# A gated linear recurrence with a squared-ReLU layer on one core: K and Q laid out in runs for the last four units, K~ and v gathered in 16-row pieces, and the chain's steps ranked first

## The chip, the core and the metric

The kernel runs on one NeuronCore of a Trainium2 chip. TensorE (PE) multiplies matrices into PSUM; VectorE (DVE) and ScalarE (ACT) work on SBUF and PSUM; GpSimd (POOL) makes masks and issues DMAs from its queue; SyncE (SP) issues DMAs. Time is what the device needs for one execution, in microseconds, as the median of several runs. The three runs of the kernel before took 705.7, 706.53 and 707.09 us; the median is 706.53.

## The reference

```python
# 4 batches, 8 heads, 768 steps, 48 columns a head
scale = np.minimum(mag, 0.999) / (mag + 1e-06)       # mag = |a_re + i a_im|
for t in range(S):
    new_re = ar * S_re - ai * S_im                    # a complex decay for each row of the state
    new_im = ar * S_im + ai * S_re
    kv = np.einsum('bhd,bhe->bhde', k[:, :, t], v[:, :, t])
    S_re, S_im = (new_re + kv, new_im)
    y[:, :, t] = np.einsum('bhd,bhde->bhe', q[:, :, t], S_re)
# the heads of a step stand side by side: x has 3072 tokens of 384
h = x @ w_in                                          # 384 x 2048
r = np.maximum(h, 0.0)
g = r * r
out = g @ w_out                                       # 2048 x 384
```

All of it is float32 to the caller; the kernel gets the two weight matrices as 64-bit words and turns them into float32 itself.

## The kernel before, in words

The 3072 steps are six units of 512 (n = 0 to 5), so a unit may begin a batch (n = 0, 3), end one (n = 2, 5), or cross from one to the next (n = 1, 4). A unit has three parts.

*The chain.* `chain(n)` turns the recurrence into attention: it scales a, multiplies it up over all steps (`inner`, `totals`, `scan`, `back`; PE turns the data with `turned`, ACT copies it out of PSUM), and `apply` makes from the running products P the rows Q~ = q P and K~ = k / P, real and imaginary part side by side, 96 numbers a head. A partition then holds four neighbouring steps (step mod 4 is c), heads and columns beside them. DVE does most of it. `gather` copies K~ by DMA from this layout into `KC`, one step a partition, four blocks of 128 steps; `load` brings v in the same way into `vv`. `places(i)` says at which partitions a block's steps stand: blocks with odd i have their two halves of 64 exchanged. From n = 2 (`EARLY`) on, all these DMAs are issued by POOL, one or two a block.

*The pairs.* `pairs(n)` takes two heads at a time, four pairs a unit. From n = 2 on, `turn` transposes Q~ and K~ on DVE (two `transpose` calls of 768 columns, in 32 x 32 blocks, written so that the 128 steps of a block stand in order of time, that is, c innermost), and twelve DMAs move the pieces into `QT`, 96 rows of columns. For n = 0 and 1, `turn_pe` does this on PE. `score` multiplies K by Q on PE for each head, block by block and in halves of 64 K steps, and DVE multiplies the result by the causal mask (`mask4`) into `As`. `keep` multiplies K~ with v (PE) and adds up the states at the block ends (ACT and DVE). `mix` adds masked scores times v and states times Q in PSUM (`ypair`); ACT copies it to `yts`, and SP's DMAs put it into `xT`, tokens in columns.

*The dense layer.* `dense(n, grp)` takes 256 tokens: PE multiplies by w_in (line L1400, `part_of`), ACT takes ReLU and square (L1431, L1432), PE multiplies by w_out (L1446 for n = 0, L1497 after it; from n = 1 on with fewer products and sums on DVE, L1512 and L1521), POOL stores the rows. In unit 0 the weights are still coming: `fetch` loads a piece (POOL's queue, L795), `convert` makes float32 of it (ACT L809 and L813, DVE L815, L819, L822).

The order of everything is planned when the program is built. `Plan.add` takes a step with its engine, an assumed duration, what it reads and writes, and a rank (smaller goes first); `Plan.order` plays this through with one free time per engine, an issue time and a latency per DMA, and emits the steps in the order that comes out. On the chip each engine runs its own list strictly in that order. Ranks: the pairs of unit n (1, n), the chain (2, n), dense work and stores (3, n), v (3, 6 + n); what empties a PSUM bank of the dense layer has (0, n). So dense work of unit n - 1 fills PE while the chain of unit n runs on DVE.

Lines that matter: L1262 the transposes, L1267 their DMAs, L1226 the gathers of K~, L892 the loads of v, L1305 the scores, L1308 the masking, L1334 and L1348 the states, L1359 and L1363 the mix, L993 the chain's turns, L1151 to L1189 `apply`.

Of the kernel before, what the change touches and what calls it, by code (L numbers as in the profile page):

```python
# [598 lines left out]
def fast_path(ctx, tc, q, k, v, a_re, a_im, moe_w_in, moe_w_out, out, flag):  # L599
# [73 lines left out]
    mask = sb("mask", 2 * C)  # L673
# [29 lines left out]
    mask4 = mask.rearrange("p (o t) -> p o t", o=2).unsqueeze(1).to_broadcast([C, W // 2, 2, C])  # L703
# [26 lines left out]
    SCORE = 0.7  # L730
    checked = []

    def step(*args, **kw):
        return plan.add(*args, **kw)
# [63 lines left out]
    def convert(i):  # L798
# [12 lines left out]
        if mixed:  # L811

            step("ACT", 1.92, keys + [("lo", i)], [("lo", i, 1)], lambda: act.activation(  # L813
                out=part(F16, 1), in_=part(I16, 3), func=AF.Copy, scale=2.0 ** -60), rank)
# [44 lines left out]
    def places(i):  # L859
        return [(CH, 0, CH), (0, CH, CH)] if i % 2 else [(0, 0, C)]  # L860

    def load(n):
# [23 lines left out]
        for i in range(W):  # L886
            b, s = divmod(n * L + i * C, S)
            src = v[b, :, s:s + C, :].rearrange("h t d -> t h d")
            for p0, t0, m in places(i):
                vrank = (CHAIN, 1) if n == 1 else (DENSE, 6 + n)  # L890
                dma(pool, [("xT", (n - (vs(n) == vs(n - 1))) % 2, NM - 1)] if n else [("gate",)], [("v", vs(n))],
                    lambda i=i, p0=p0, t0=t0, m=m, src=src: pool.dma_start(  # L892
                        out=t[p0:p0 + m, i], in_=src[t0:t0 + m]), vrank, m * 1536, 4.0,
                    group=n)

    def chain(n):
# [90 lines left out]
        def turned(src, put, by, keys, rk):  # L987
# [6 lines left out]
            step("PE", 0.12 * NM, keys, [(b,)], go, rk)  # L994
# [125 lines left out]
        check("DVE", 0.16, [("tot",)], [("lv", n)], level, ahead)  # L1120
# [93 lines left out]
    def gather(n, z, p, np):  # L1214
# [5 lines left out]
        for i in needs(n):  # L1220
            for p0, t0, m in places(i):
                queue = sp if n < EARLY and i % 2 else pool
                t0, m4 = 32 * i + t0 // W, m // W
                dma(queue, keys, [(k_, z, q_) for q_ in range(p, p + np)
                                  for k_ in ("KC", "KC%d" % (i == 3))],
                    lambda i=i, p0=p0, t0=t0, m=m, m4=m4, queue=queue: queue.dma_start(  # L1226
                        out=kc[p0:p0 + m, i], in_=nat[t0:t0 + m4]),
                    rank, m * w * 4, group=(n, p))

# [10 lines left out]
    def pairs(n, which):  # L1240
# [9 lines left out]
        def turn(i):  # L1250
# [5 lines left out]
            for j in range(2):  # L1256
                nat = ff[z][:, j * Z:(j + 1) * Z].rearrange(
                    "p (c h j r) -> p c h j r", c=W, h=HH, j=NJ)[:, :, ts(i % 2, 2)]
                dst = T6[:, i % 2].rearrange("p j (k h t c) -> p k c h j t", k=2, h=2, c=W)
                step("DVE", tt(768), [("f", z, 2 * j), ("f", z, 2 * j + 1)],  # L1260
                     [("a", z) if i % 2 == 0 else ("qk", z)],
                     lambda nat=nat, dst=dst, j=j: dve.transpose(out=dst[:, j], in_=nat), rank)  # L1262
# [28 lines left out]

        def score(i, h):
            s = got["T", i]
            T = QT[s].rearrange("p (i k h t) -> p i k h t", i=W, k=2, h=2)[0:R]
            b = "sc%d" % take("sc", 2)
            sa = bank[b].rearrange("p (j t) -> p j t", j=W)
# [3 lines left out]
            def go():  # L1300
                for j0 in range(0, W, 2):
                    for half in range(2):
                        for j in (j0, j0 + 1):
                            p0, t0 = CH * (half ^ (j % 2)), CH * half
                            pe.matmul(sa[p0:p0 + CH, j, t0:C], lhsT=T[:, j, 1, h, t0:t0 + CH],  # L1305
                                      rhs=T[:, j, 0, h, t0:C], start=True, stop=True)
            step("PE", SCORE, [("QT", s, h)], [(b,)], go, rank, slack=True)
            step("DVE", tt(L) + 0.05, [(b,)], [("A", a)], lambda: dve.tensor_tensor(  # L1308
                out=As[a].rearrange("p (j o t) -> p j o t", o=2, t=C),
                in0=bank[b].rearrange("p (j o t) -> p j o t", o=2, t=C), in1=mask4,  # L1310
                op=ALU.mult), rank)

        def keep(i):
# [10 lines left out]
            for js in ([j for j in need if j < 3], [j for j in need if j == 3]):  # L1324
# [14 lines left out]
                for j in js:  # L1339
# [6 lines left out]
                    else:  # L1346
                        step("DVE", tt(2 * D) + 0.04, reads, writes,
# [3 lines left out]
        def mix(i):  # L1351
            T = QT[got["T", i]].rearrange("p (i k h t) -> p i k h t", i=W, k=2, h=2)[0:R]
# [3 lines left out]
            def go():  # L1356
                for j in range(W):
# [331 lines left out]
```

## Time and profile before

| | |
|---|---|
| median of three runs | 706.53 us |
| profiled execution, its own time | 706.77 us |
| its span | 705.0 us |
| mean granted clock of TensorE | 0.991 |
| PE, DVE, ACT, POOL busy | 630.2, 557.3, 339.5, 96.3 us |
| DMAs that POOL issues for K~ (L1226) and v (L892, both forms) | 52 and 36 |
| mean DMA traffic | 113 GB/s |

The profile is of one execution. A group of instructions is shown by line, engine, operation and shape, with its busy time, the mean duration of one in nanoseconds, and the idle time of its engine just before it with what ended it. PE's matmuls overlap, so their single durations are longer than their distance; a float32 matmul stands in the profile as two passes, so that one `matmul` call of the code counts as two instructions. The chain that ended last gives starts, lengths and lines in order of time. Waits are listed as who waited for whom, the microseconds in total, how often, and the longest.

### The profile page before, as it was taken

The numbers are of one execution on the slowest core, as the hardware profiler recorded it, in microseconds if no ns is written. First come the engines' busy times: TensorE is split into PE (matmuls) and PEld (weight loads), VectorE is DVE, ScalarE is ACT, GpSimd is POOL, SyncE is SP. The second block draws the span as 40 slices with busy tenths as digits, with TensorE's granted clock in tenths as the row PEclk, the third lists the DMA queues.
The fourth block names the chain that finished last, engine by engine and source line by source line (L and its number), as shares of the span: only waits on it lengthen the run. The fifth ranks groups of instructions, "written<-read, shape, count | busy, mean of one in ns | idle before, by whom it ended". The sixth has DMA issues, their size and how long they took to land.

```text
span 705.0 us, 11855 instructions
## 1 busy us (share of the span) xinstructions
PE 630.2 (89%) x4442; PEld 559.2 (79%) x4442; DVE 557.3 (79%) x1125; ACT 339.5 (48%) x586; POOL 96.3 (14%) x166
## 2 busy tenths in 40 slices
PE   0108898999999999989999999999999999999996
PEld 0007775686778999978998898988899988999996
DVE  7999992989787897885999698988887998336721
ACT  6678736865675153336453438435247352032230
POOL 6301140201100010120021030011030011032200
PEclk9999999999999999999999999999999999999999
DMA  9924386111630006562027580045561035287600
GB/s 285 332 99 101 68 224 191 24 45 45 169 98 5 12 16 156 145 168 68 13 66 185 138 178 8 1 101 146 135 164 18 23 92 141 51 279 253 240 3 27
DMA packets 52068, 79.53 MB, mean 113 GB/s; under 512 B 7745, under 2 KB 35073, under 8 KB 52001
## 3 DMA queue, kind: packets, MB, share of 16 engines
q0 software_dynamic: 11712, 40.90, 19.2%
q1 hardware_dynamic: 36160, 32.79, 18.8%
q10 hardware_dynamic: 4128, 4.98, 2.8%
q8 instruction: 37, 0.61, 0.4%
q14 instruction: 31, 0.25, 0.1%
HBM read 48.76 MB, written 4.72 MB: 76 GB/s over the span
## 4 chain that ended last, share of the span: by engine, by line
PE 61%; DVE 26%; DMA 6%; ACT 3%; issue 2%; SPq 1%; ACTq 0%; DVEq 0%
PE d L1400 21%; PE d L1497 20%; PE d L1446 5%; DVE aq L1262 4%; PE sc L1305 4%; DVE f L1189 3%; DMA aq<-in_q_dram 3%; DVE f L1151 3%; PE yp L1359 3%; PE tr L1334 2%; PE yp L1363 2%; DVE g L1512 2%; DVE aq L1155 2%; DVE KC L1038 1%; DMA QT<-aq 1%
## 5 line engine op out<-in xcount | busy, mean ns | idle before, releaser
L1400 PE MATMUL d<-xT,w 128*128 128x256 f32 x1056 | 237.7, 382 | 2.9 <-DMA xT<-yt 2.9
L1400 PEld LDWEIGHTS d<-xT,w 128*128 128x128 f32 x1056 | 199.6, 191 | 30.6 <-DMA xT<-yt 3.3
L1497 PE MATMUL d<-w,g 128*128 128x192 f32 x832 | 144.2, 329 | 0.0
L1497 PEld LDWEIGHTS d<-w,g 128*128 128x128 f32 x832 | 136.0, 191 | 2.1 <-issue 1.3
L1431 ACT ACTIVATE g<-d 128x512 f32<-128x512 f32 x88 | 52.4, 596 | 129.0 <-PE d L1400 111.2
L1432 ACT ACTIVATE g<-g 128x512 f32<-128x512 f32 x96 | 60.6, 631 | 3.0
L1512 DVE TENSOR_TENSOR g<-g 128x512 f32<-128x512 f32 x56 | 37.7, 687 | 30.6 <-ACT g L1432 18.6
L1497 PE MATMUL d<-T,g 128*128 128x192 f32 x336 | 59.6, 330 | 0.0
L1497 PEld LDWEIGHTS d<-T,g 128*128 128x128 f32 x336 | 56.0, 193 | 0.3
L1226 POOL DMA_DIRECT2D KC<-f x52 | 27.6, 545 | 174.9 <-DVE f L1189 125.3
L1458 POOL DMA_DIRECT2D out_dram<-ot x22 | 12.3, 559 | 278.1 <-DVE ot L1521 247.4
L1446 PE MATMUL d<-w,g 128*128 128x384 f32 x128 | 45.5, 505 | 3.1 <-DVE w L822 3.1
L1262 DVE STREAM_TRANSPOSE aq<-f 128x768 f32<-128x768 f32 x32 | 47.5, 1573 | 0.3
L1151 DVE TENSOR_TENSOR f<-aq,xn 128x384 f32<-128x384 f32 (+1 forms) x64 | 45.5, 749 | 1.4 <-ACT xn L1102 1.4
L1371 ACT COPY yt<-yp 112x512 f32<-112x512 f32 x24 | 13.9, 581 | 63.1 <-PE yp L1363 55.7
L1308 DVE TENSOR_TENSOR A<-sc,mask 128x512 f32<-128x512 f32 x45 | 29.8, 685 | 12.5 <-PE sc L1305 12.2
L1446 PEld LDWEIGHTS d<-w,g 128*128 128x128 f32 x128 | 24.4, 197 | 18.7 <-DVE w L822 3.7
L1305 PEld LDWEIGHTS sc<-QT 96*64 96x64 f32 x736 | 34.1, 137 | 5.6 <-issue 3.3
L1305 PE MATMUL sc<-QT 96*64 96x128 f32 (+1 forms) x736 | 37.4, 250 | 0.6 <-DMA QT<-aq 0.3
L964 DVE TENSOR_TENSOR f<-aq 128x384 f32<-128x384 f32 x72 | 36.9, 552 | 0.8
L1521 DVE TENSOR_TENSOR ot<-ot,d 128x192 f32<-128x192 f32 x61 | 20.7, 348 | 20.0 <-PE d L1497 19.7
L1359 PE MATMUL yp<-A,v 128*48 128x128 f32 x320 | 32.4, 277 | 3.5 <-DVE A L1308 3.3
(179 smaller groups left out, 919.5 us busy)
## 6 DMA issues: line engine op xcount, KB each, us to landing
QT<-aq SPq DMA_DIRECT2D x128, 64.0 KB, 2.0
f<-in_moe_w_in_dram POOLq DMA_DIRECT2D x8, 768.0 KB, 6.8
f<-in_moe_w_out_dram POOLq DMA_DIRECT2D x8, 768.0 KB, 6.8
out_dram<-ot POOLq DMA_DIRECT2D x22, 192.0 KB, 2.4
QT<-aq ACTq DMA_DIRECT2D x64, 64.0 KB, 2.1
KC<-f POOLq DMA_DIRECT2D x36, 96.0 KB, 3.4
xT<-yt SPq DMA_DIRECT2D x36, 96.0 KB, 2.6
aq<-in_a_re_dram SPq DMA_DIRECT2D x8, 384.0 KB, 4.1
```

The costliest lines, as they stand in the source:

```text
L964: lambda c=c, j=j: dve.tensor_tensor(out=f[j], in0=a[:, :, :, c - 1], in1=a[:, j, :, c].unsqueeze(1).to_broadcast([C, 2, HH, D]), op=ALU.m ...
L1151: lambda j=j, r=r: dve.tensor_tensor(out=f4[:, j, r], in0=a[:, r], in1=over(j), op=ALU.mult), late[z])
L1262: lambda nat=nat, dst=dst, j=j: dve.transpose(out=dst[:, j], in_=nat), rank)
L1305: pe.matmul(sa[p0:p0 + CH, j, t0:C], lhsT=T[:, j, 1, h, t0:t0 + CH], rhs=T[:, j, 0, h, t0:C], start=True, stop=True)
L1308: step("DVE", tt(L) + 0.05, [(b,)], [("A", a)], lambda: dve.tensor_tensor(out=As[a].rearrange("p (j o t) -> p j o t", o=2, t=C), in0=bank[ ...
L1359: pe.matmul(ypair[64 * h:64 * h + D, ts(j, C)], lhsT=v5[:, j, 2 * i + h], rhs=aa[h][:, j], start=True, stop=at[j] is None)
L1400: pe.matmul(ps, lhsT=w1[:, f // FP, m, ts(f % FP, C)], rhs=xT[:, n % 2, m, ts(grp, G)], start=(m == 0), stop=(m == NM - 1))
L1431: act.activation(out=o, in_=ps, func=AF.Relu)
L1432: act.activation(out=o, in_=o, func=AF.Square)
L1446: pe.matmul(ps, lhsT=gt[:, f % 2, ts(i, C)], rhs=w2[:, f], start=(f == 0), stop=(f == NF - 1))
L1497: pe.matmul(bank[b][:, 0:DH], lhsT=g4[:, r, j], rhs=w(j), start=first and j == 0, stop=last and j == NT - 1)
L1512: step("DVE", tt(4 * C), gk(x0, h) + gk(x1, h), gk(o, h), lambda: dve.tensor_tensor(out=g4[:, o, sl], in0=g4[:, x0, sl], in1=g4[:, x1, sl] ...
```

## The change

For n = 2 to 5, `turn` writes Q of a head as (c, t), where t is step div 4 and c is step mod 4, 32 neighbouring numbers at a time, and K as (half, c, 16 steps), 16 neighbouring numbers at a time, with K first and one `transpose` for each of its two heads. PE reads K as it stands, so the rows of a score block are in K's new order, and reads Q with a step of 32 columns, so that the columns of scores and outputs stay in order of time (`columns`). v and the gathered K~ must stand in K's order too: `places` now gives eight pieces of 16 rows a block, each a DMA of its own. A second mask in that order is made once, by four matmuls of the first mask with a permutation (`swap`, `causal`) and a copy on ACT; for n = 2 to 5 the masking uses it. Steps of `apply`, `totals`, `back`, `turned` and `keep` that are not DVE's get rank (-1, n), ahead of all else, except the pairs of n = 0. Nine planned durations change (masking, conversion on ACT, the chain's turns, `level`, `mix`, scores, the states' sums, ReLU and square, w_out's products); they alter the order alone.

```diff
@@ -670,7 +670,8 @@
...
     perm = sb("perm", C)
-    mask = sb("mask", 2 * C)
+    masks = sb("mask", 4 * C)
+    mask = masks[:, 0:2 * C]
     NS = 14
...
@@ -700,7 +701,12 @@
...
                                fill=0.0, base=-(p0 ^ (CH * o)), channel_multiplier=-1)
-    mask4 = mask.rearrange("p (o t) -> p o t", o=2).unsqueeze(1).to_broadcast([C, W // 2, 2, C])
+    TQ = CH // W
+    swap = As[0][:, C:2 * C]
+    pool.tensor_copy(out=swap.rearrange("p (o c t) -> p o t c", o=2, c=W),
+                     in_=ident.rearrange("p (o t c) -> p o t c", o=2, c=W))
+    mask4 = [m.rearrange("p (o t) -> p o t", o=2).unsqueeze(1).to_broadcast([C, W // 2, 2, C])
+             for m in (mask, masks[:, 2 * C:4 * C])]
     dve.memset(ypair, 0.0)
...
@@ -727,11 +733,15 @@
...
     SUM = 0.22
-    SCORE = 0.7
+    SCORE = 0.72
     checked = []
 
-    def step(*args, **kw):
-        return plan.add(*args, **kw)
+    FIRST = ("apply", "totals", "back", "turned", "keep")
+
+    def step(eng, dur, reads, writes, fn, rank, *args, **kw):
+        if eng != "DVE" and any(x in fn.__qualname__ for x in FIRST) and rank >= (PAIR, 1):
+            rank = (-1, rank[1])
+        return plan.add(eng, dur, reads, writes, fn, rank, *args, **kw)
 
...
@@ -856,8 +866,10 @@
...
 
-    def places(i):
-        return [(CH, 0, CH), (0, CH, CH)] if i % 2 else [(0, 0, C)]
+    def places(i, n):
+        if n >= EARLY:
+            return [(CH * (o ^ (i % 2)) + TQ * c, c, TQ * o, TQ) for o in range(2) for c in range(W)]
+        return [(CH, 0, 0, CH), (0, 0, CH, CH)] if i % 2 else [(0, 0, 0, C)]
 
...
@@ -885,12 +897,14 @@
...
             b, s = divmod(n * L + i * C, S)
-            src = v[b, :, s:s + C, :].rearrange("h t d -> t h d")
-            for p0, t0, m in places(i):
-                vrank = (CHAIN, 1) if n == 1 else (DENSE, 6 + n)
-                dma(pool, [("xT", (n - (vs(n) == vs(n - 1))) % 2, NM - 1)] if n else [("gate",)], [("v", vs(n))],
-                    lambda i=i, p0=p0, t0=t0, m=m, src=src: pool.dma_start(
-                        out=t[p0:p0 + m, i], in_=src[t0:t0 + m]), vrank, m * 1536, 4.0,
+            src = v[b, :, s:s + C, :]
+            vrank = (CHAIN, 1) if n == 1 else (DENSE, 6 + n)
+            src = (src.rearrange("h (c t) d -> c t h d", c=1) if n < EARLY else
+                   src.rearrange("h (t c) d -> c t h d", c=W))
+            for p0, c, t0, m in places(i, n):
+                dma(pool, [("xT", (n - (vs(n) == vs(n - 1))) % 2, NM - 1)] if n else [("gate",)],
+                    [("v", vs(n))], lambda i=i, p0=p0, t0=t0, m=m, c=c, src=src: pool.dma_start(
+                        out=t[p0:p0 + m, i], in_=src[c, t0:t0 + m]), vrank, m * 1536, 4.0,
                     group=n)
...
@@ -1218,16 +1232,30 @@
...
         for i in needs(n):
-            for p0, t0, m in places(i):
+            for p0, c, t0, m in places(i, n):
                 queue = sp if n < EARLY and i % 2 else pool
-                t0, m4 = 32 * i + t0 // W, m // W
+                if n >= EARLY:
+                    src = nat[32 * i + t0:32 * i + t0 + m, c]
+                else:
+                    src = nat[32 * i + t0 // W:32 * i + (t0 + m) // W]
                 dma(queue, keys, [(k_, z, q_) for q_ in range(p, p + np)
                                   for k_ in ("KC", "KC%d" % (i == 3))],
-                    lambda i=i, p0=p0, t0=t0, m=m, m4=m4, queue=queue: queue.dma_start(
-                        out=kc[p0:p0 + m, i], in_=nat[t0:t0 + m4]),
+                    lambda i=i, p0=p0, m=m, src=src, queue=queue: queue.dma_start(
+                        out=kc[p0:p0 + m, i], in_=src),
                     rank, m * w * 4, group=(n, p))
...
 
+
+    def causal():
+        for o in range(2):
+            for p0 in (0, CH):
+                pe.matmul(bank["tr0"][p0:p0 + CH, ts(o, C)],
+                          lhsT=swap[:, p0 ^ (CH * o):(p0 ^ (CH * o)) + CH], rhs=mask[:, 0:C],
+                          start=True, stop=True)
+
+    step("PE", 0.6, [("A", 0)], [("tr0",)], causal, (CHAIN, -1))
+    step("ACT", ac(2 * C), [("tr0",)], [("mask",)], lambda: act.copy(
+        out=masks[:, 2 * C:4 * C], in_=bank["tr0"][:, 0:2 * C]), (CHAIN, 0.2))
 
...
@@ -1253,13 +1281,18 @@
...
             T6 = aq[z].rearrange("p (y j x) -> p y j x", y=2, j=NJ)
-            for j in range(2):
+            for j in (1, 0):
                 nat = ff[z][:, j * Z:(j + 1) * Z].rearrange(
-                    "p (c h j r) -> p c h j r", c=W, h=HH, j=NJ)[:, :, ts(i % 2, 2)]
-                dst = T6[:, i % 2].rearrange("p j (k h t c) -> p k c h j t", k=2, h=2, c=W)
-                step("DVE", tt(768), [("f", z, 2 * j), ("f", z, 2 * j + 1)],
-                     [("a", z) if i % 2 == 0 else ("qk", z)],
-                     lambda nat=nat, dst=dst, j=j: dve.transpose(out=dst[:, j], in_=nat), rank)
+                    "p (c h j r) -> p c h j r", c=W, h=HH, j=NJ)
+                parts_ = [(nat[:, :, ts(i % 2, 2)], T6[:, i % 2].rearrange(
+                    "p j (k h c t) -> p k c h j t", k=2, h=2, c=W)[:, 0])] if not j else [
+                    (nat[:, :, 2 * (i % 2) + h], T6[:, i % 2].rearrange(
+                        "p j (k h o c t) -> p k h c j o t", k=2, h=2, o=2, c=W)[:, 1, h])
+                    for h in range(2)]
+                for src, dst in parts_:
+                    step("DVE", tt(384 if j else 768), [("f", z, 2 * j), ("f", z, 2 * j + 1)],
+                         [("a", z) if i % 2 == 0 else ("qk", z)],
+                         lambda src=src, dst=dst: dve.transpose(out=dst, in_=src), rank)
             for b in range(W):
...
@@ -1289,11 +1322,16 @@
...
 
+        def columns(s):
+            t6 = QT[s].rearrange("p (i k h %s) -> p i k h t c" % ("t c" if n < EARLY else "c t"),
+                                 i=W, k=2, h=2, c=W)[0:R]
+            return t6[:, :, 0], QT[s].rearrange("p (i k h t) -> p i k h t", i=W, k=2, h=2)[0:R, :, 1]
+
         def score(i, h):
             s = got["T", i]
-            T = QT[s].rearrange("p (i k h t) -> p i k h t", i=W, k=2, h=2)[0:R]
+            qt, kt = columns(s)
             b = "sc%d" % take("sc", 2)
-            sa = bank[b].rearrange("p (j t) -> p j t", j=W)
+            sa = bank[b].rearrange("p (j t c) -> p j t c", j=W, c=W)
             a = take("A", 3 if 0 < n < ROOM else 2)
...
@@ -1301,13 +1339,13 @@
...
                         for j in (j0, j0 + 1):
-                            p0, t0 = CH * (half ^ (j % 2)), CH * half
-                            pe.matmul(sa[p0:p0 + CH, j, t0:C], lhsT=T[:, j, 1, h, t0:t0 + CH],
-                                      rhs=T[:, j, 0, h, t0:C], start=True, stop=True)
+                            p0, t0 = CH * (half ^ (j % 2)), CH // W * half
+                            pe.matmul(sa[p0:p0 + CH, j, t0:], lhsT=kt[:, j, h, ts(half, CH)],
+                                      rhs=qt[:, j, h, t0:], start=True, stop=True)
             step("PE", SCORE, [("QT", s, h)], [(b,)], go, rank, slack=True)
-            step("DVE", tt(L) + 0.05, [(b,)], [("A", a)], lambda: dve.tensor_tensor(
+            step("DVE", tt(L), [(b,), ("mask",)], [("A", a)], lambda: dve.tensor_tensor(
                 out=As[a].rearrange("p (j o t) -> p j o t", o=2, t=C),
-                in0=bank[b].rearrange("p (j o t) -> p j o t", o=2, t=C), in1=mask4,
+                in0=bank[b].rearrange("p (j o t) -> p j o t", o=2, t=C), in1=mask4[n >= EARLY],
                 op=ALU.mult), rank)
...
@@ -1344,12 +1382,13 @@
...
                     else:
-                        step("DVE", tt(2 * D) + 0.04, reads, writes,
+                        step("DVE", tt(2 * D), reads, writes,
                              lambda o=o, j=j, ps=ps: dve.tensor_tensor(
...
         def mix(i):
-            T = QT[got["T", i]].rearrange("p (i k h t) -> p i k h t", i=W, k=2, h=2)[0:R]
+            qt, _ = columns(got["T", i])
+            y4 = ypair.rearrange("p (j t c) -> p j t c", j=W, c=W)
             at, s = got["S", i]
...
@@ -1360,9 +1399,9 @@
...
                         if at[j] is not None:
-                            pe.matmul(ypair[64 * h:64 * h + D, ts(j, C)], lhsT=at[j][:, h],
-                                      rhs=T[:, j, 0, h], start=False, stop=True)
-            step("PE", 2.0, [("A", got["A", i, h]) for h in range(2)]
+                            pe.matmul(y4[64 * h:64 * h + D, j], lhsT=at[j][:, h],
+                                      rhs=qt[:, j, h], start=False, stop=True)
+            step("PE", 1.68, [("A", got["A", i, h]) for h in range(2)]
                  + [("v", vs(n)), ("QT", got["T", i], 0), ("QT", got["T", i], 1),
```

More of the change, by code (lines that the diff above doesn't have):

```diff
@@ L811, in convert @@
         if mixed:
[L813 removed]
+            step("ACT", 1.65, keys + [("lo", i)], [("lo", i, 1)], lambda: act.activation(
                 out=part(F16, 1), in_=part(I16, 3), func=AF.Copy, scale=2.0 ** -60), rank)
@@ L1119, in level @@
                               scalar2=None, op0=ALU.mult)
-        check("DVE", 0.16, [("tot",)], [("lv", n)], level, ahead)
+        check("DVE", 0.26, [("tot",)], [("lv", n)], level, ahead)
         def squares(j):
@@ L1432, in relu @@
                 act.activation(out=o, in_=o, func=AF.Square)
-            step("ACT", 2 * ac(2 * G), [(b, "x"), (b,), (b, "y")],
+            step("ACT", 2 * ac(2 * G) + 0.1, [(b, "x"), (b,), (b, "y")],
                  [(b,)] + [("g", s, r) for r in range(4)], relu, (0, n))
```

4 lines of the change are left out of this document (2 added, 2 removed).

## The prediction

> **What bounds the kernel now.** I read the page first: span, busy shares, and the 40 slices.
>
> ```profile
> span 705.0 us, 11855 instructions
> PE 630.2 (89%) x4442; PEld 559.2 (79%) x4442; DVE 557.3 (79%) x1125; ACT 339.5 (48%) x586; POOL 96.3 (14%) x166
> PE   0108898999999999989999999999999999999996
> ```
>
> TensorE (PE) hardly works in the first three slices (the first chain runs on VectorE), and is nearly full from there to the end. So after about 58 us only three things can move the end: PE's amount of work, PE's idle time, and its clock. The table by stages says how much idle time there is (second pair of numbers: PE busy; the column PEclk: granted clock).
>
> ```profile
> 58.00:140.00 82.00, 75.61 (x535) 58.41 (x534) 66.83 (x118) 54.80 (x89) 14.54 (x21) 0.98 0.51 129
> 140.00:300.00 160.00, 159.18 (x1144) 137.69 (x1144) 134.03 (x290) 82.70 (x153) 13.85 (x26) 1.00 0.29 77
> 300.00:320.00 20.00, 17.11 (x163) 14.96 (x160) 16.46 (x29) 7.74 (x12) 5.08 (x7) 0.93 0.72 175
> 380.00:400.00 20.00, 17.96 (x196) 15.96 (x195) 13.56 (x25) 9.03 (x16) 0.00 (x0) 1.00 0.63 156
> 460.00:500.00 40.00, 37.35 (x293) 33.17 (x292) 32.70 (x42) 17.95 (x31) 4.77 (x9) 0.98 0.52 131
> 500.00:580.00 80.00, 80.00 (x525) 74.34 (x525) 72.89 (x146) 39.94 (x70) 8.90 (x14) 0.99 0.31 80
> 580.00:600.00 20.00, 18.42 (x200) 16.51 (x199) 16.95 (x28) 3.95 (x7) 2.12 (x4) 1.00 0.56 137
> ```
>
> In the units that the change touches (n = 2 to 5, from about 260 us on) PE is idle for 2.89 + 2.04 + 2.65 + 1.58 = 9.2 us; the clock below 1 costs another 0.07 x 20 + 0.02 x 40 + 0.01 x 80 = 3.0 us. Between 58 and 140 us it is 6.4 idle and 1.6 of clock. That is all that a faster VectorE (DVE) can give back: about 12 us. Who ends these waits is in the list of waits and in PE's timeline:
>
> ```profile
> PE yp L1359 <- DVE A L1308: 3.3, 5, 1.6
> PE d L1446 <- DVE w L822: 3.1, 1, 3.1
> PE d L1400 <- DMA xT<-yt: 2.9, 1, 2.9
> PE tr L1334 <- ACT St L1344: 2.6, 2, 1.7
> ```
>
> **The transposes.** Groups of instructions by shape; behind the first bar stand their busy us and the mean ns of one:
>
> ```profile
> L1262 DVE STREAM_TRANSPOSE aq<-f 128x768 f32<-128x768 f32 x32 | 47.5, 1573 | 0.3
> L1189 DVE TENSOR_TENSOR f<-f,aq 128x768 f32<-128x768 f32 x16 | 14.6, 951 | 0.1
> L1082 DVE TENSOR_TENSOR KC<-e,yt 128x384 f32<-128x384 f32 x24 | 12.3, 551 | 0.2
> L1087 DVE TENSOR_TENSOR xn<-KC 128x384 f32<-128x384 f32 x12 | 9.7, 810 | 0.4
> L1226 POOL DMA_DIRECT2D KC<-f x52 | 27.6, 545 | 174.9 <-DVE f L1189 125.3 <-issue 21.5 <-PE sc L1305 18.3
> L892 POOL DMA_DIRECT2D v<-in_v_dram x30 | 22.8, 767 | 38.9 <-issue 35.3 <-DMA g<-in_moe_w_in_dram 2.3 <-DMA w<-in_moe_w_in_dram 1.3
> L813 ACT ACTIVATE w<-w 128x768 f16<-128x768 int16 x5 | 9.4, 1926 | 0.0
> L822 DVE CUSTOM_DVE_ANT_0 w<-T,w 128x1536 uint16<-128x1536 uint16 x5 | 4.8, 959 | 0.3
> ```
>
> A transpose of 768 columns (L1262) takes 1573 ns where other DVE work of that size takes 951; its destination has the mod-4 step innermost, so consecutive elements land four floats apart. L1087 shows the same thing without a transpose: 384 elements written 16 floats apart take 810, against 551 (L1082) written in a row. So a far-stepped write costs (1573 - 951)/768 = 0.81 or (810 - 551)/384 = 0.67 ns an element. After the change Q is written in runs of 32 and K in runs of 16: I take 0.95 us for Q and two of 0.55 for K (one instruction more per pair), 2.05 instead of 3.15 us a pair: 1.1 us less, 4.4 a unit, 17.6 over 16 pairs. Bounds: no gain, if transposing itself is the 1573, and 17.6. They are on DVE's path to scores and sums, so each unit's pairs can end some 4 us sooner. The DMAs into QT (12 of 64 KB a pair, on SP and ACT) are as many as before, and wait for all three transposes.
> The Trainium skill ("SBUF — State Buffer", section "Door 1: The DMA port swizzle") says that SBUF has 16-byte lines, and that an access that goes to a new line pays. The two strided rows agree for DVE's writes.
>
> **Reading Q by PE.** Scores and state products now read Q 32 floats apart inside each four; PSUM is written in natural order. No row shows PE reading far-stepped data. Bounds: nothing, or DVE's surcharge. PE's strided side that is in the trace, L1285, writes PSUM four floats apart:
>
> ```profile
> 169.65 0.87 PE tr L1285 x8
> 402.43 1.34 PE sc L1305 x32
> ```
>
> Eight passes of 128 columns in 0.87 us are 0.85 ns a column, no more than the 0.84 of the contiguous products below. I take nothing, as it is the same engine; the other end is priced with the rivals. The page's rule names no engine, and speaks for that other end.
>
> **POOL's queue.** A gather of K~ was 1 or 2 DMAs a block, now 8: 4, 6, 4, 4 issues per half of the heads become 24, 32, 24, 24, so 36 become 208; v goes from 24 to 128. At 545 and 767 ns that is 172 x 0.545 + 104 x 0.767 = 174 us more on an engine busy for 96. The bytes stay. What waits behind them:
>
> ```profile
> 262.99 2.23 POOL L1226 DMA_DIRECT2D KC<-f  x4 [11.07 <-issue]
> 283.48 2.18 POOL L1226 DMA_DIRECT2D KC<-f  x4 [18.26 <-PE sc L1305]
> 363.51 3.13 POOL L1226 DMA_DIRECT2D KC<-f  x6 [3.97 <-DVE f L1189]
> KC<-f POOLq DMA_DIRECT2D x36, 96.0 KB, 3.4
> KC<-f POOLq DMA_DIRECT2D x16, 192.0 KB, 3.3
> 310.07 2.86 PE L1400 MATMUL d<-xT,w 128*128 128x256 f32 x12
> 408.24 10.60 PE d L1497 x64
> ```
>
> The work behind the last K~ is sums and the last mix; I give it the 5.8 us that now lie between the last score (402.43, above) and the end of the last mix (408.2, where w_out's products go on). n = 3 is the tightest: 363.5 + 32 x 0.545 = 381 for the first half of the heads, 398.4 for the second, landed by 401.8, last mix over at 407.6: just within what it is now. For n = 2 the second half lands at 283.5 + 24 x 0.545 + 3.4 = 300, its last mix is over at 306, now at 310.1; n = 4 and 5 have as many issues as n = 2. So nothing is lost against now, and only part of DVE's 4 us can be cashed in n = 3. The cover is DVE's own work on the second half and PE's dense products; without it the 13 to 17 us of a half would stand on the path. v is issued one unit ahead, 24.5 us in which POOL has little else (one store of a row block may wait behind it): covered, with one exception.
>
> **The exception: v of n = 2.** In the built order its 32 issues stand ahead of the last five fetches of w_out (QT, QT, w, T, T), which wait behind them.
>
> ```profile
> 89.31 4.65 POOL L892 DMA_DIRECT2D v<-in_v_dram  x6 [6.00 <-issue]
> 93.95 1.44 POOL L795 DMA_DIRECT2D QT<-in_moe_w_out_dram  x2
> QT<-in_moe_w_out_dram POOLq DMA_DIRECT2D x2, 768.0 KB, 10.3
> 111.40 7.90 PE L1446 MATMUL d<-w,g 128*128 128x384 f32 x24
> 122.43 4.54 PE L1446 MATMUL d<-w,g 128*128 128x384 f32 x8 [3.13 <-DVE w L822]
> 250.25 19.43 PE d L1400 x90
> ```
>
> The first fetch slips from 93.95 to 89.3 + 24.5 = 113.8, lands by about 124, and is converted by two steps on ACT and two on DVE (L813 1.93, L822 0.96, and two shorter ones): some 4 us, 128. PE needed that piece at 119.3 and got it at 122.4. The built order now gives PE 24 passes of L1400 ahead of it (19.43/90 each: 5.2 us, to 124.5), where 12 stood behind it before. Before, 119.3 to 129.4 held 20 passes worth 5.2 us, 5 us lost; after, a wait of 2 to 4 us and some clock. I take 0, bounds -2 to +4.
>
> **The ranks and the rest.** The chain's PE and ACT steps go ahead of others; the built order shows it in unit 0, where the second half's L1172 to L1189 move ahead of two conversion steps. PE waits 1.14 us there:
>
> ```profile
> 81.99 2.14 PE L1285 MATMUL d<-ident,f 128*96 128x128 f32 x16 [1.14 <-DVE f L1189]
> 315.82 4.62 PE L1400 MATMUL d<-xT,w 128*128 128x256 f32 x13 [2.89 <-DMA xT<-yt]
> 5.21 0.84 ACT L914 ACTIVATE f<-aq 128x768 f32<-128x768 f32 x1 [3.12 <-DMA aq<-in_a_re_dram]
> ```
>
> I take -1 (bounds 0 and -1.5). The second mask adds a copy on POOL, four matmuls on an idle PE, and an ACT copy at the head of ACT's queue, where everything of ACT waits behind it; ACT waits for a_re until 5.21 anyway: 0, at worst +0.7. Every score's masking now also waits for that copy, done 250 us earlier. The changed planned times add no instruction; they only order.
> Units 2 to 5: the stalls inside the pairs (2.04 + 2.65 + 1.58 and the clock's 1.6 beside them, 7.9) are waits for masking, sums and QT, which DVE now delivers some 4 us sooner in each unit; I let them go but for a rest of 1, and the late one is then K~ on POOL. The 2.89 at 315.8 is the way from the last mix through yt to xT; the built order still leaves PE no w_out product behind the last mix of n = 2, and now none in n = 5 either (16 matmuls before): one such wait stays, one of 2.9 comes. Net -7.9 + 1 + 2.9 = -4. Bounds: -12.2 (all goes) and +5.8 (nothing goes, two such waits come).
>
> **Sum.** 705.0 + 0 - 1 - 4 = 700 us of span. The profiled execution was 706.77, 1.8 over its span, and 0.2 over the median 706.53: 701.5 us.
>
> **The rivals.**
> (1) PE reads Q slowly. Columns of n = 2 to 5: 32 scores of 16 passes, 1536 columns, and 112 state products of two passes of 128: 77,800. Two stand side by side (the row of 1.34 us has 32 passes of 96 columns on average, 0.44 ns each), so half of it counts: 38,900 x 0.67 to 0.81 = 26 to 32 us, all on a full PE: 728 to 734. For it: two strided DVE rows. Against: PE's own strided row is free. By the page's line rule the same columns pay, and the time is this rival's. 0.2.
> (2) POOL becomes the bound, the other way round. If 16-row gathers cost v's 767 instead of 545 ns, n = 3's last K~ lands at 363.5 + 64 x 0.767 + 3.4 = 416, its last mix ends at 422 instead of 408, 13 us later, with only 24 passes of L1497 left over in the built order (10.60/64 each: 4 us); the other units lose their gain: 705 - 1 + 9 + 1.8 = 715. It decides from 0.56 us an issue on (408.2 - 5.8 - 3.4 - 363.5 = 35.5 over 64). For it: v's DMAs, in small pieces, do take 767. Against: 545 holds for 96 as for 192 KB, and K~'s rows stay in one piece each. 0.14.
> (3) The transposes do not get faster, or the fixed order keeps PE's stalls where they are: 705 to 708. 0.12.
> The forecast: 0.54.
>
> **The numbers.** Own range of the likeliest: 705 + 1.5 - 12.2 - 1.5 - 2 = 691 at best; its unfavourable bounds lead into (3). The range 692 to 716 takes in (3) and (2), and leaves out (1) and the extremes. Within 0.2% (1.4 us) is what this kernel's measurement can hardly tell from no change. Faster: 0.54 and a third of (3), 0.58; same 0.09; slower: (1), (2) and a part of (3), 0.33.
>
> **What would show it.** Transposes at 0.95 and 0.55 us (if not: the step on DVE is wrong). L1305's and L1363's successors at 1.34 us per 32 passes as before (if above 2: rival 1). POOL near 270 us busy, gathers at 545 ns, v at 767, K~ of n = 3 landed some 38 us after its first issue. PE's idle time from 300 to 600 near 5 instead of 9.2 us, with waits left for xT and KC. From 110 to 140 us PE loses as much as now. Wrong would be any price on PE's reads, and any wait that a slow POOL makes at the sums.

## The result

The changed kernel takes 731.28 us (median of four runs, 729.03 to 734.33), against 706.79 us for the kernel before beside it: the ratio is 1.035, with a 95% interval of 1.0318 to 1.0382. It is slower by 3.5%, where 701.5 us was predicted. The profiled execution took 730.35 us, with a span of 728.6.

The page of the changed kernel, its busy shares and PE's 40 slices:

```profile
span 728.6 us, 12280 instructions
PE 660.5 (91%) x4450; PEld 575.3 (79%) x4450; DVE 544.5 (75%) x1141; ACT 339.8 (47%) x587; POOL 227.0 (31%) x443
PE   0008899999999999989999999999999999999996
```

DVE has 12.8 us less to do and POOL 130.7 us more, but neither is what grew with the span: PE is busy for 30.3 us more with eight instructions more (the second mask), and the span is 23.6 longer. The table by stages (length, then busy us of PE, its weight loads, DVE, ACT and POOL; granted clock, DMA share, GB/s) shows that PE has hardly any idle time left where it had most:

```profile
58.00:140.00 82.00, 77.59 (x554) 60.77 (x553) 71.48 (x136) 57.66 (x97) 27.18 (x48) 1.00 0.53 128
140.00:300.00 160.00, 159.51 (x1102) 136.42 (x1101) 123.63 (x272) 80.36 (x146) 33.45 (x67) 1.00 0.28 78
300.00:320.00 20.00, 19.40 (x171) 16.08 (x171) 13.68 (x25) 4.37 (x7) 5.10 (x10) 1.00 0.35 89
320.00:340.00 20.00, 18.52 (x90) 16.03 (x89) 16.42 (x54) 14.66 (x30) 12.20 (x24) 1.00 0.51 116
340.00:500.00 160.00, 160.00 (x1065) 144.04 (x1064) 131.24 (x257) 72.41 (x129) 69.26 (x141) 1.00 0.37 89
500.00:620.00 120.00, 120.00 (x832) 107.03 (x833) 91.34 (x186) 46.26 (x82) 46.15 (x93) 1.00 0.33 84
```

From 300 to 620 us PE is idle for 0.6 + 1.5 = 2.1 us, and its clock is 1.00 throughout. The stalls went as hoped, and more so. What takes longer is PE's own work, and the groups by shape say which. First the kernel before, then the changed kernel:

```profile
L1305 PE MATMUL sc<-QT 96*64 96x128 f32 x368 | 34.2, 279 | 0.6 <-DMA QT<-aq 0.3 <-ACT QT L1288 0.2
L1305 PE MATMUL sc<-QT 96*64 96x64 f32 x368 | 27.2, 221 | 0.0
L1363 PE MATMUL yp<-QT,St 96*48 96x128 f32 x248 | 25.7, 272 | 0.0
L1359 PE MATMUL yp<-A,v 128*48 128x128 f32 x320 | 32.4, 277 | 3.5 <-DVE A L1308 3.3
...
L1343 PE MATMUL sc<-QT 96*64 96x128 f32 x368 | 52.5, 371 | 0.0
L1343 PE MATMUL sc<-QT 96*64 96x64 f32 x368 | 35.9, 272 | 0.0
L1402 PE MATMUL yp<-QT,St 96*48 96x128 f32 x248 | 36.2, 359 | 0.0
L1398 PE MATMUL yp<-A,v 128*48 128x128 f32 x320 | 34.4, 280 | 2.0 <-DVE A L1346 2.0
L1295 DVE STREAM_TRANSPOSE aq<-f 128x384 f32<-128x384 f32 x32 | 16.9, 554 | 0.2
L1295 DVE STREAM_TRANSPOSE aq<-f 128x768 f32<-128x768 f32 x16 | 15.1, 942 | 0.0
```

The two groups that read Q as moving data (scores L1343, state products L1402) have longer passes; the masked scores times v (L1398), which stand between the state products and read contiguously, hardly change (280 ns against 277). The chain that ended last (start, length, work) shows it beside a place where Q is still read contiguously:

```profile
414.46 0.57 PE yp L1398 x8
415.04 0.45 PE yp L1402 x4
415.48 0.22 PE yp L1398 x4
416.83 2.75 PE sc L1343 x32
...
168.25 0.82 PE sc L1343 x16
```

At 168 us unit 1 still reads Q contiguously: 16 passes in 0.82 us, as in the kernel before. At 416.8, with the step of 32 floats, 32 passes take 2.75 us, where the kernel before needs 1.34. Four passes of a state product take 0.45 us beside 0.22 for four passes of as many columns (128) that read contiguous data.

### The profile page after: what moved, and what is told of

Same layout as the page of the kernel before. It is cut to its first block, busy times and chain, and to the rows that moved or that the text cites. A ratio compares the mean times of both kernels' runs of the same rounds, so it can differ in the third digit from the quotient of the medians.

```text
span 728.6 us, 12280 instructions
## 1 busy us (share of the span) xinstructions
PE 660.5 (91%) x4450; PEld 575.3 (79%) x4450; DVE 544.5 (75%) x1141; ACT 339.8 (47%) x587; POOL 227.0 (31%) x443
## 4 chain that ended last, share of the span: by engine, by line
PE 85%; DVE 10%; DMA 2%; ACT 1%; issue 1%; SPq 0%; DVEq 0%; ACTq 0%
PE d L1439 30%; PE d L1536 27%; PE sc L1343 7%; PE d L1485 5%; PE yp L1402 4%; PE tr L1372 3%; PE yp L1398 3%; PE tr L1439 1%; PE sc L1439 1%; DMA aq<-in_a_im_dram 1%; PE tr L1318 1%; PE tr L1007 1%; DVE f L978 1%; DVE A L1346 1%; PE d L1318 1%
## 5 line engine op out<-in xcount | busy, mean ns | idle before, releaser
L1439 PE MATMUL d<-xT,w 128*128 128x256 f32 x1056 | 234.6, 380 | 3.8 <-issue 2.2
L1243 POOL DMA_DIRECT2D KC<-f x224 | 108.0, 490 | 116.6 <-DVE f L1203 76.8
L1536 PEld LDWEIGHTS d<-w,g 128*128 128x128 f32 x832 | 135.3, 190 | 4.2 <-issue 3.9
L906 POOL DMA_DIRECT2D v<-in_v_dram x134 | 71.8, 543 | 32.2 <-issue 8.7
L1343 PE MATMUL sc<-QT 96*64 96x128 f32 (+1 forms) x736 | 59.9, 321 | 0.0
L1343 PEld LDWEIGHTS sc<-QT 96*64 96x64 f32 x736 | 46.9, 148 | 11.3 <-issue 1.8
L1398 PE MATMUL yp<-A,v 128*48 128x128 f32 x320 | 34.4, 280 | 2.0 <-DVE A L1346 2.0
L1402 PE MATMUL yp<-QT,St 96*48 96x128 f32 x248 | 36.2, 359 | 0.0
```

Source lines behind the costliest of these rows:

```text
L906: [("v", vs(n))], lambda i=i, p0=p0, t0=t0, m=m, c=c, src=src: pool.dma_start(out=t[p0:p0 + m, i], in_=src[c, t0:t0 + m]), vrank, m * 1536 ...
L1243: lambda i=i, p0=p0, m=m, src=src, queue=queue: queue.dma_start(out=kc[p0:p0 + m, i], in_=src),
L1343: pe.matmul(sa[p0:p0 + CH, j, t0:], lhsT=kt[:, j, h, ts(half, CH)], rhs=qt[:, j, h, t0:], start=True, stop=True)
L1398: pe.matmul(ypair[64 * h:64 * h + D, ts(j, C)], lhsT=v5[:, j, 2 * i + h], rhs=aa[h][:, j], start=True, stop=at[j] is None)
L1402: pe.matmul(y4[64 * h:64 * h + D, j], lhsT=at[j][:, h], rhs=qt[:, j, h], start=False, stop=True)
L1439: pe.matmul(ps, lhsT=w1[:, f // FP, m, ts(f % FP, C)], rhs=xT[:, n % 2, m, ts(grp, G)], start=(m == 0), stop=(m == NM - 1))
```

## The experiments

Theory A: PE pays for reading Q 32 floats apart. Theory B: the loss comes from POOL's 16-row pieces, the permuted K, or the order of the work. Each ratio is to the kernel before, run beside that kernel; its median was 705.1 to 707.6 us.

**Only Q's layout put back.** Every engine's list of instructions is that of the changed kernel, in the same order; only access patterns differ.

```diff
-                    "p j (k h c t) -> p k c h j t", k=2, h=2, c=W)[:, 0])] if not j else [
+                    "p j (k h t c) -> p k c h j t", k=2, h=2, c=W)[:, 0])] if not j else [
...
-            t6 = QT[s].rearrange("p (i k h %s) -> p i k h t c" % ("t c" if n < EARLY else "c t"),
+            t6 = QT[s].rearrange("p (i k h %s) -> p i k h t c" % "t c",
```

> Exactly the changed kernel's instructions in the same order on every engine; only Q's layout in QT is put back (the transpose of Q writes it four floats apart, PE reads it contiguous). K's permuted steps, the second mask, POOL's small pieces and the ranks stay. Theory A (PE pays for reading Q 32 floats apart): the 22 us of scores and 14 us of state products go, 32 passes of a score take 1.34 to 1.5 us again, the time is 698 to 708 us. Theory B (the loss comes from POOL's many pieces, from the permuted K or from the order): 725 to 735 us, as the changed kernel.

Measured: 695.88 us, ratio to the kernel before 0.9829 (0.9792 to 0.9866), 35 us below the changed kernel and 2 us under theory A's range. From its page, groups and chain:

```profile
PE 630.0 (91%) x4450; PEld 560.6 (81%) x4450; DVE 550.6 (79%) x1141; ACT 340.0 (49%) x587; POOL 227.0 (33%) x443
L1343 PE MATMUL sc<-QT 96*64 96x128 f32 x368 | 35.1, 287 | 0.0
L1402 PE MATMUL yp<-QT,St 96*48 96x128 f32 x248 | 25.8, 272 | 0.0
404.18 1.34 PE sc L1343 x32
```

POOL is as busy as in the changed kernel, the permuted K and the order are there, and PE is back at 630.0 us. So theory B falls for the loss, and everything else in the change together is worth 1.7% to the good.

**Q contiguous on both sides, the step moved to PSUM.** PE reads Q's columns in the order in which they lie, and writes each to its place:

```diff
-            sa = bank[b].rearrange("p (j t c) -> p j t c", j=W, c=W)
+            sa = bank[b].rearrange("p (j t c) -> p j c t" if n >= EARLY else "p (j c t) -> p j c t",
+                                   j=W, c=W)
...
-                            pe.matmul(sa[p0:p0 + CH, j, t0:], lhsT=kt[:, j, h, ts(half, CH)],
-                                      rhs=qt[:, j, h, t0:], start=True, stop=True)
...
+                            pe.matmul(sa[p0:p0 + CH, j, :, t0:], lhsT=kt[:, j, h, ts(half, CH)],
+                                      rhs=qt[:, j, h, :, t0:], start=True, stop=True)
```

(`columns` and the `y4` of the mix likewise; units 0 and 1 keep contiguous reads and writes.)

> The changed kernel with Q contiguous in QT, as it has it, and also read contiguously: the columns of scores and state products go through PE in the order (step mod 4, step) and are written to PSUM four floats apart, which puts them in natural order there. Same instructions, same order. Theory A with a free PSUM side: 696 to 703 us, the time that was predicted for the change. Theory A, but PSUM steps cost as much as the reads: 726 to 736 us. Theory B: about 731 us, with scores at 1.34 to 1.5 us per 32 passes.

Measured: 696.07 us, ratio 0.9828 (0.9802 to 0.9855); PE is busy for 628.7 us, and the passes of units 2 to 5 are back at 278 and 221 ns. Steps of four floats in PSUM cost nothing that shows here. DVE's transposes are at 0.94 and 0.55 us again, which makes 8 us of DVE less than in the run above (542.6 against 550.6), and the time is the same.

**The stepped read alone, in the kernel before.**

```diff
-                dst = T6[:, i % 2].rearrange("p j (k h t c) -> p k c h j t", k=2, h=2, c=W)
+                dst = T6[:, i % 2].rearrange(
+                    "p j (k h t c) -> p k c h j t" if j else "p j (k h c t) -> p k c h j t",
+                    k=2, h=2, c=W)
...
-                                      rhs=T[:, j, 0, h, t0:C], start=True, stop=True)
+                                      rhs=qt[:, j, h, t0:], start=True, stop=True)
```

(`qt` comes from `columns`, as in the changed kernel.)

> The kernel before with one part of the change alone: Q is written contiguous by its transpose and read 32 floats apart by PE, from the third unit on. K, v, the mask, POOL's pieces and the ranks are as before. Theory A: PE's scores and state products cost 30 to 36 us more, DVE's Q transposes 0.6 us a pair less: 730 to 742 us. Theory B: 700 to 707 us.

Measured: 735.33 us, ratio 1.038 (1.0349 to 1.0411). The engines' lists are those of the kernel before, in the same order, and the scores' passes take 370 ns instead of 279. One part of the change makes the whole loss, without POOL's pieces (POOL 96.2 us busy) and without the ranks.

**The price by itself.** Fourteen groups of 16 products (32 passes) of 128 columns behind the changed kernel's last addition, reading one buffer in different orders; three of them (L1640, L1648 and L1650 of its profile):

```diff
+            for k in range(16):
+                pe.matmul(bank["sc0"][CH * (k % 2):][0:CH, 0:C], lhsT=ident[0:R, 0:CH], rhs=ident[0:R], start=True, stop=True)
...
+                pe.matmul(bank["sc0"][CH * (k % 2):][0:CH, 0:C], lhsT=ident[0:R, 0:CH], rhs=ident[0:R].rearrange("p (a b) -> p b a", b=32), start=True, stop=True)
+            for k in range(16):
+                pe.matmul(bank["sc0"][CH * (k % 2):][0:CH, 0:C], lhsT=ident[0:R, 0:CH], rhs=ident[0:R].rearrange("p (a b r) -> p b a r", a=4, r=2), start=True, stop=True)
```

> The changed kernel with 14 groups of 16 extra products behind its last addition, each 128 columns wide and of 64 columns of weights, read from the same 96 rows with different steps; the total time means nothing here. Two side by side, contiguous: 32 passes of 128 columns at 0.44 ns, 1.8 us a group. Theory A by a shared read rate: 32 floats apart 3.6 us side by side, and alone, where a contiguous group takes 3.5 us, no more than that. Theory A by a surcharge on each column: alone 3.5 plus at least 1.8 us. If the 16-byte line decides, step 2 costs half of the surcharge, steps 4, 8 and 32 all of it, runs of 4 floats none, runs of 2 half. Steps in PSUM (4 and 32) as contiguous. Theory B: no group differs from the contiguous one.

PE's timeline of it (start, length, line); the distance to the next start is the time of a group. It is one execution:

```profile
724.59 1.97 PE L1640 MATMUL sc<-ident 96*64 96x128 f32 x32
726.38 2.00 PE L1642 MATMUL sc<-ident 96*64 96x128 f32 x32
728.22 3.88 PE L1644 MATMUL sc<-ident 96*64 96x128 f32 x32
731.93 3.91 PE L1646 MATMUL sc<-ident 96*64 96x128 f32 x32
735.65 3.86 PE L1648 MATMUL sc<-ident 96*64 96x128 f32 x32
739.31 2.02 PE L1650 MATMUL sc<-ident 96*64 96x128 f32 x32
741.14 1.93 PE L1652 MATMUL sc<-ident 96*64 96x128 f32 x32
742.89 1.93 PE L1654 MATMUL sc<-ident 96*64 96x128 f32 x32
744.63 1.93 PE L1656 MATMUL sc<-ident 96*64 96x128 f32 x32
746.38 1.93 PE L1658 MATMUL sc<-ident 96*64 96x128 f32 x32
748.15 3.66 PE L1660 MATMUL sc<-ident 96*64 96x128 f32 x32
751.64 7.23 PE L1662 MATMUL sc<-ident 96*64 96x128 f32 x32
758.70 7.27 PE L1664 MATMUL sc<-ident 96*64 96x128 f32 x31
...
765.83 3.12 PE L1666 MATMUL sc<-ident 96*64 96x128 f32 x31
```

| group | read or written | us a group |
|---|---|---|
| L1640 | contiguous, two side by side | 1.79 |
| L1642 | step of 2 floats | 1.84 |
| L1644, L1646, L1648 | step of 4, 8, 32 floats | 3.71, 3.72, 3.66 |
| L1650, L1652, L1654 | runs of 2, 4, 8 floats, then a jump | 1.83, 1.75, 1.74 |
| L1656, L1658 | contiguous, PSUM written 4 and 32 floats apart | 1.75, 1.77 |
| L1660 | contiguous, one at a time | 3.49 |
| L1662 | step of 32 floats, one at a time | 7.06 |
| L1664 | step of 4 floats, one at a time, at a granted clock of 0.50 | 7.1 |

L1666, the fourteenth group, is contiguous and two side by side once more. From 757.9 to 768.1 us the granted clock was 0.50, over all of L1664 and most of L1666; up to there it was 1.00, so that L1662 had 0.94 on average. In that stretch L1666 needs 3.12 us where L1640 needs 1.97, but L1664 takes no longer than L1662. So L1664 can't be set beside the 3.49 of L1660, and as far as one group shows, the halved clock does not lengthen a read that is already stepped.

Side by side and at full clock, a column costs twice as much as soon as no two neighbours lie in the same 16 bytes, and no more for a longer step. With two columns to 16 bytes nothing is paid; my expectation of half the price for steps and runs of two was wrong. Side by side and alone (L1662) the factor is two, so it is not one reader shared by two products: alone, a column takes (7.06 - 3.49) us / 4096 = 0.87 ns more, as much as a contiguous one takes altogether. The Trainium skill ("Advanced Engine Details and Errata", section "SBUF Cachelines") has 16-byte lines in SBUF and asks for at least two hits on a line; the table agrees on both counts. Its next section, "PSUM Cachelines", says that any non-contiguous access to PSUM slows matmuls significantly; 1.75 and 1.77 against 1.79 us say that such writes are free here.

**Pairs of floats in the real kernel.** The changed kernel with Q as (c div 2, t, c mod 2):

```diff
-                parts_ = [(nat[:, :, ts(i % 2, 2)], T6[:, i % 2].rearrange(
-                    "p j (k h c t) -> p k c h j t", k=2, h=2, c=W)[:, 0])] if not j else [
+                parts_ = [(nat.rearrange("p (a b) h j r -> p b a h j r", b=2)[:, b, :, ts(i % 2, 2)],
+                           T6[:, i % 2].rearrange("p j (k h a t b) -> p k b a h j t", k=2, h=2,
+                                                  a=2, b=2)[:, 0, b]) for b in range(2)] if not j else [
...
+                  q[:, :, 0].rearrange("p i h (a t b) -> p i h t a b", a=2, b=2))
```

> The changed kernel with the four steps of Q in QT in two pairs: (step mod 4 over 2, 32 steps, step mod 2). PE reads two neighbouring floats, then two 64 floats on, and writes PSUM in order; Q's transpose becomes two instructions of half the size that write 8 bytes apart. Theory A in the form that the probe gives (a column is dear only where each one lies in another 16-byte piece; two columns to a piece cost nothing): scores back at 278 and 221 ns a pass, 694 to 700 us. Theory A' (every jump costs; the probe's small buffer hid it): half of the price, 710 to 718 us.

Measured: 694.9 us, ratio 0.9845 (0.9799 to 0.9892). Its groups:

```profile
L1345 PE MATMUL sc<-QT 96*64 96x128 f32 x368 | 34.3, 281 | 0.0
L1404 PE MATMUL yp<-QT,St 96*48 96x128 f32 x248 | 25.8, 275 | 0.0
L1296 DVE STREAM_TRANSPOSE aq<-f 128x384 f32<-128x384 f32 x64 | 33.2, 554 | 0.6
```

PE still jumps 64 floats after every second column, and pays nothing. DVE's transposes that write 8 bytes apart (half of this row) take the 554 ns of those that write in runs of 16 floats.

**Where the other 1.7% come from.** Four runs on the parts that are not the read. The first has the kernel before with the ranks and the planned times alone:

```diff
+    FIRST = ("apply", "totals", "back", "turned", "keep")
...
+            rank = (-1, rank[1])
...
-    SCORE = 0.7
+    SCORE = 0.72
```

> The kernel before with the chain's steps ranked first and the changed planned times, and no other part of the change: layouts, transposes, K~ and v pieces as before. The changed kernel without the stepped reads stood 11 us below the kernel before (695.9 against 707.6); this run says where the 11 came from. Theory O (the new order of the work brings them): 695 to 700 us. Theory K (the cheaper transposes of K and K~ in small pieces bring them): 704 to 708 us. In between, both have a share.

Measured: 703.63 us, ratio 0.9977 (0.994 to 1.0014): the order by itself cannot be told from no change. Theory O falls; the time lies just under theory K's range. The planned times alone (`FIRST = ()` in the same kernel):

> The kernel before with the changed planned times alone: no ranks, no layouts. Theory O by the ranks: 704 to 709 us. Theory O by the planned times: 695 to 700 us. Theory K: 704 to 708 us.

Measured: 710.31 us, ratio 1.0073 (1.0043 to 1.0102), slower than any theory said. The kernel with PSUM's steps, with its ranks taken off (`FIRST = ()`):

> The kernel with Q contiguous on both sides and PSUM written in steps, with the chain's steps at their old ranks (the planned times stay changed). Theory O, by the ranks: 701 to 708 us. Theory O, by the planned times, or theory K: 695 to 699 us.

Measured: 700.17 us, ratio 0.9937 (0.9913 to 0.996), between the two ranges. And the order-only kernel with Q contiguous and PSUM stepped, but K, K~ and v as before:

> The order-only kernel, and Q contiguous in QT, read contiguously and put in natural order by PSUM's steps; K, K~ and v as in the kernel before, so POOL is busy for some 96 us and not 227. Theory O: 694 to 699 us, about the order-only kernel, as DVE's 10 us less lie beside a full PE. Theory K: 703 to 707 us.

Measured: 692.83 us, ratio 0.9846 (0.9805 to 0.9887), below both ranges. The four fit together: the ranks give 1% with the old layouts (0.9977 / 1.0073) and with the new (0.9828 / 0.9937); the planned times cost 0.7%; another 1.3 to 1.5% go with cheaper transposes on top of the order, whichever of the two is made cheaper, K's (first experiment, 5.5 us of DVE saved, with the small pieces of K~ and v and the permuted K beside it), Q's (this one, 8.7 us) or both (0.9828). The first two experiments have the same lists in the same order and stand 8 us of DVE apart, and take the same time: there DVE's last 8 us are not cashed in. So neither theory K nor theory O was right alone. In the list of waits, all that PE is said to wait for after 58 us in the last run is this (total, times, longest):

```profile
PE d L1461 <- DVE w L826: 1.7, 2, 0.9
PE tr L1346 <- DMA KC<-f: 1.3, 1, 1.3
PE sc L1415 <- DVE w L826: 0.9, 2, 0.5
PE tr L1346 <- ACT St L1356: 0.4, 1, 0.4
PE yp L1371 <- DVE A L1320: 0.3, 1, 0.3
```

**A better version?** The last kernel beats the kernel before and the changed one, with POOL as idle as before (96.6 us). It was run again beside a version of itself whose planner knows the measured times of the transposes:

```diff
-                step("DVE", tt(768), [("f", z, 2 * j), ("f", z, 2 * j + 1)],
+                step("DVE", 1.55 if j else 0.93, [("f", z, 2 * j), ("f", z, 2 * j + 1)],
```

> The order-only kernel with Q contiguous and PSUM stepped once more, beside the one with the measured planned times: 0.981 to 0.989 of the kernel before again.

> The order-only kernel with Q contiguous and PSUM stepped, and the planned times of the two transposes of a pair set to those measured (0.93 and 1.55 us, planned so far at 0.87 each); it only moves the order. If the order is near its best, 691 to 696 us; if DVE's planned times mattered, 686 to 690 us.

Measured: 697.35 us, ratio 0.9863 (0.9817 to 0.991), as expected; and 697.67 us, ratio 0.988 (0.9842 to 0.9918), no gain, and above both figures given for it. The versions between 0.983 and 0.988 cannot be ranked by these intervals.

The repeat says one thing more. It is the same kernel text, but its trace has another order: on DVE the first difference comes at 77 us. There the first build has a product of `apply` (L1193, 76.94 us) before a state's sum (L1360, 78.48), and the repeat has the sum first (77.06, then 77.23). `Plan.order` keeps the engines' names in a set and takes the first of several with equal times, so that ties fall as the set happens to be ordered, which need not be the same in two builds. That can turn an order over without a change in the text, and so a few tenths of a per cent between kernels built once may be the build's order. The repeat's list on DVE is that of the order-only run, so that these two differ in Q's layout and PSUM's steps alone: 8.6 us of DVE less, PE's idle time from 300 to 600 us down from 4.8 to 2.2 us (9.2 in the kernel before), and 1.1% of the time (0.9863 / 0.9977). The runs on Q's reads do not suffer from this: the first two have the changed kernel's lists in its order, and the third that of the kernel before.

## Why the prediction was wrong

The step that failed is the one headed "Reading Q by PE": between its two bounds, nothing and DVE's surcharge, I took nothing, "as it is the same engine", and the price came out at the other bound or above it. The row it rested on (L1285) is a step on PE's write side, in PSUM, and says nothing of its reads from SBUF; the probe shows the two to differ, free on the one side and double on the other. The two rows of DVE, writes of a different engine but to the same memory, were the nearer ones. So it is rival (1), to which I gave 0.2, and its signs are there: 2.75 us per 32 passes, above the 2 that I named.

Even rival (1)'s price was at best just high enough. I put 38,900 columns at 0.67 to 0.81 ns, 26 to 32 us. The step from 1.34 to 2.75 us is 1.41 us for 32 x 96 / 2 = 1536 columns that count, 0.92 ns each, 35.7 us for all. The changed kernel and the first experiment stand 731.3 - 695.9 = 35 us apart in their medians, 32.6 us in the spans of the two profiled executions. That rival (1)'s 728 to 734 holds the 731.3 is partly luck, two errors that cancel: the price is at the upper end of what I said or some us above it, and the rest of the change came out 5.6 us better than the forecast (695.9 against 701.5).

The other steps:

- *Transposes.* Predicted 0.95 and 0.55 us, measured 0.942 and 0.554. Right, and so rival (3), in which they do not get faster or PE's stalls stay, is out. What they bring to the time is told with the experiments.
- *Units 2 to 5.* Predicted -4 us. Without the read price, in the first experiment, PE's idle time from 300 to 600 us is 2.3 us instead of 9.2 (with 1.8 more from 600 to 640, where the kernel before has none), and the clock is at 1.00: about 10 us with the 3.0 of clock, near my bound of -12.2 for all of it going. The waits for xT, which I put at 2.9 more than before, are 2.3 us in all in the first experiment, and 1.0 in the changed kernel, which idles another 1.5 us at 321.9, at the place of the old wait, with no releaser named.
- *Ranks.* I gave them -1 us, in unit 0 alone. The runs say 1% of the time, some 7 us, and that the planned times, which I gave nothing, take 0.7%, some 5 us, back.
- *POOL.* Predicted near 270 us busy at 545 and 767 ns an issue; measured 227.0 at 490 and 543 on average:

```profile
L1243 POOL DMA_DIRECT2D KC<-f x224 | 108.0, 490 | 116.6 <-DVE f L1203 76.8 <-PE d L1439 11.8 <-ACT T L823 10.5
L906 POOL DMA_DIRECT2D v<-in_v_dram x134 | 71.8, 543 | 32.2 <-issue 8.7 <-DMA v<-in_v_dram 6.3 <-PE yp L1398 5.8
364.41 8.60 POOL L1243 DMA_DIRECT2D KC<-f  x18 [0.31 <-DVE f L1203]
...
386.32 11.94 POOL L1243 DMA_DIRECT2D KC<-f  x25 [0.55 <-DMA KC<-f]
KC<-f POOLq DMA_DIRECT2D x208, 24.0 KB, 2.6
```

  The cheaper issues did not make n = 3 earlier, since POOL waits between them, for transfers among others: its 64 gathers run from 364.4 to 398.3, 530 ns each, and the last one lands at about 400.9, where I had 401.8. That is under the 0.56 us an issue from which rival (2) decides. Rival (2) is out: PE's waits for KC come to 1.4 us in all.
- *v of n = 2.* The slip of w_out's first fetch came as worked out:

```profile
113.37 1.45 POOL L805 DMA_DIRECT2D QT<-in_moe_w_out_dram  x2
...
119.37 2.75 PE L1439 MATMUL d<-xT,w 128*128 128x256 f32 x12
122.81 2.86 PE L1439 MATMUL d<-xT,w 128*128 128x256 f32 x12 [0.69 <-ACT g L1470]
126.29 2.85 PE L1485 MATMUL d<-w,g 128*128 128x384 f32 x8 [0.62 <-DVE w L832]
```

  113.4 instead of my 113.8, and the 24 passes of the other product stand ahead as the built order had them. But the waits behind them are 0.6 to 0.7 us, not 2 to 4, and the clock stays at 1.00. From 58 to 140 us PE's idle time fell from 6.4 to 4.4 us and the clock's 1.6 us went too, where I had expected the ranks' 1 us alone.

What stays open: the 1.1 to 1.5% that go with the cheaper transposes on top of the order are 8 to 11 us. For Q's that is about what DVE saves, but in the first experiment it is more than K's transposes save (5.5 us). Part may be the clock, which was 0.92 from 58 to 100 us in the order-only run and 1.00 in the first experiment; but the order-only kernel with Q contiguous and PSUM stepped had 0.92 there too, in both its runs. Part may be the small pieces or the order of the build. The intervals are too wide to settle it.

## What to carry to other kernels

A layout change moves the price of a step from a writer to a reader, and the reader has to be priced by a row of its own side and memory: a free step in PSUM says nothing of SBUF. When two orders must meet on a full PE, keep its SBUF reads in runs of at least 8 bytes and let it write the step into PSUM. And before taking a large reordering, run it with the old access patterns: the same list of instructions showed at once that all the rest was a gain.

## What the runs showed of the hardware

- PE's moving float32 data at full clock: 0.85 ns a column alone and 0.44 side by side as long as two neighbours share 16 bytes, twice that if not, whatever the step (4, 8 or 32 floats side by side; 32 alone). At a granted clock of 0.50 one group with a step of 4, alone, took 7.1 us, no more than 7.06 for a step of 32 at 0.94.
- DVE's transposes, when they write, are dear and cheap at the same steps: 8 bytes apart 554 ns for 384 columns, as in runs; 16 bytes apart 1566 for 768 (the first experiment), against 942.
- PSUM writes 16 and 128 bytes apart cost PE nothing (1.75 and 1.77 us against 1.79).
- POOL's issue of a DMA became cheaper as the piece became smaller, by the means of these groups: 490 ns with 16 rows of K~ against 545 with 64 and 128, 543 against 767 for v.
